# Splitting each weight load of a DeltaNet and hard-swish MLP kernel into two transfers by partition

## The chip, the core and the metric

The kernel runs on one core of one Trainium2 chip. The metric is the device time of one execution in microseconds (us), and the time that counts is the median over several executions. A core has five engines that run side by side, each with its own queue of instructions: TensorE (PE, matrix products; PEld is its loading of the stationary operand), VectorE (DVE), ScalarE (ACT), GpSimd (POOL) and SyncE (SP). SP computes nothing here: it issues transfers between the chip's memory (HBM) and the on-chip buffer, and 16 DMA engines carry them out. The on-chip buffer has 128 partitions; a tile's first dimension lies across them.

## The reference

The inputs `q`, `k`, `v` have 4 batches, 8 heads, 768 positions and 48 features; `beta` has one number for each batch, head and position. The two weight matrices are 64-bit floats: `moe_w_in` is 384 x 2048 and `moe_w_out` is 2048 x 384.

```python
k_n = k / (np.linalg.norm(k, axis=-1, keepdims=True) + 1e-06)
for t in range(S):                                   # per batch and head
    y[:, :, t] = einsum('bhd,bhde->bhe', q[:, :, t], state)
    v_old = einsum('bhde,bhd->bhe', state, k_n[:, :, t])
    state = state + bt * einsum('bhd,bhe->bhde', k_n[:, :, t], v[:, :, t] - v_old)
x = y.transpose(0, 2, 1, 3).reshape(3072, 384)
h = x @ w_in
out = (h * np.clip(h + 3.0, 0.0, 6.0) / 6.0) @ w_out
```

## The kernel before

The recurrence is done in 24 chunks of 32 positions. The four batches of a chunk share the 128 partitions, so a load of a chunk of `k`, `q` or `v` is four transfers of 32 partitions (`load_k`, `load_q`, `load_v`, lines 168, 180 and 193; 48 KB each, in runs of 192 bytes). For each chunk `prep` normalises the keys, turns keys and queries (line 524, evicted by ACT at line 532) and makes the products of keys and queries (line 547, masked by DVE at line 558). A triangular system is solved for the first chunk by small products (`product`, line 596) and for later groups of four chunks by elimination on DVE (lines 730 and 735) that `join` completes (lines 684 to 710). `chain` then carries the state from chunk to chunk. Every two chunks make a block of 256 tokens for the MLP: `up` (line 994) and later `up_by_eleven` (line 1066) multiply by `w_in`, `down` (line 1162) and `down_by_seven` (line 1226) by `w_out`.

The weights arrive as 64-bit floats that no engine multiplies, so they are loaded raw and converted on the chip. They come in 16 pieces, eight of `w_in` and eight of `w_out`. A piece is 128 partitions of 768 numbers, 768 KB raw, and lies on a partition in three runs of 2,048 bytes (`w_in`) or two of 3,072 (`w_out`). `load_w` (line 331) brings one to a raw place: a part of the tile `spare`, or a part of `w_out` that is not yet filled. `scales` (line 356) rebuilds the exponents in four ACT instructions for each piece, and `convert` (lines 378, 383 and 389) does the rest in three DVE instructions. Raw places are used again, so from piece 6 on a load waits until the piece that held its place has been read (`frees`).

The order of all instructions of the first part is written out by hand in the string `ORDER`: `w` stands for the next weight piece, `k`, `q` and `v` for the next transfer of such a load, `a` for the next ACT step of `scales`, `c` for the next DVE step of `convert`. SP issues transfers in this order, one after the other. Each transfer tells of its landing by one of eight semaphores that are handed out in turn, and a semaphore is not used again before its last transfer has landed. So SP stops at a transfer until the one eight places before it (with ACT's own transfers counted) has landed. Around the first pieces the order on SP is: piece 0, six transfers of keys, piece 1, six transfers of keys and queries, piece 2, six more, piece 3, seven more, piece 4. The capital words `K`, `Q`, `V`, `W`, which `do` would hold back behind the last PE instruction, stand in no place of `ORDER`.

```python
320  def load_w(i):
...
331      nc.sync.dma_start(
332          out=raws[i].rearrange("p s f z -> p s (f z)"), in_=src.bitcast(U32)
333      )
...
356  nc.scalar.activation(out=z, in_=z if n else d.bitcast(I16)[:, :, :, 3], func=func, ...)
```

Of the kernel before, what the change touches and what calls it, by code (L numbers as in the profile page):

```python
# [10 lines left out]
U32 = mybir.dt.uint32  # L11
# [33 lines left out]
def kernel(  # L45
# [21 lines left out]
    nc = tc.nc  # L67
# [27 lines left out]
    def rows(b):  # L95
        return slice(C * b, C * b + C)
# [4 lines left out]
    def group(t):  # L101
        return (0, t) if t < G0 else ((t - G0) // GS + 1, (t - G0) % GS)
# [34 lines left out]
    def needs(*what):  # L137
        assert past.issuperset(what), (what, set(what) - past)
# [74 lines left out]
    for j, value in enumerate((1.0, -1.0)):  # L213
        m = mask2[:, j, :]
        for b in range(B):
            nc.gpsimd.memset(mask2[rows(b), j, :], value)
            nc.gpsimd.affine_select(
                out=mask2[rows(b), j, :], in_=mask2[rows(b), j, :], pattern=[[1, C]],
# [95 lines left out]
    raws = []  # L314
    for i, n in enumerate((0, 1, 2, 3, 4, 5, 0, 1, 3, 4, 5, 0, 1, 5, 0, 1)):
        s, f = weights[i][0].shape[1:]
# [3 lines left out]
    def load_w(i):  # L320
        dst, src = weights[i]
        if src.dtype == FP32:
            if i >= NWI:
                needs(("w", NWI - 1))
            nc.sync.dma_start(out=dst, in_=src)
            past.add(("raw", i))
            return
        if i in frees:
            needs(("seen", frees[i], 0), ("seen", frees[i], 1))
        past.add(("raw", i))  # L330
        nc.sync.dma_start(
            out=raws[i].rearrange("p s f z -> p s (f z)"), in_=src.bitcast(U32)
        )

    es = [
        spare[:, 2, j : j + WP * NKT // 2].bitcast(U16).rearrange("p (s f) -> p s f", s=NKT)
# [1016 lines left out]
    def made(name, make, ok=True):  # L1353
        if name not in gens:
            gens[name] = make() if ok else iter(())
        return gens[name]

    def prep_of(t):
        return made(("p", t), lambda: prep(t), t < N)
# [7 lines left out]
    def inverse_of(g):  # L1367
        return made(
            ("i", g), lambda: halves_of(g) if g == 1 else inverse(g), g < NG
        )  # L1370
# [6 lines left out]
    def pieces():  # L1377
        for i in range(NW):
            load_w(i)
            yield  # L1380
# [37 lines left out]
    def behind_tensor(ins):  # L1418
        last = next(
            i for i in reversed(nc.cur_bb.bb.instructions) if i.engine == mybir.EngineType.PE  # L1420
        )
        tc.add_manual_dep(
            ins, last.name,
            mybir.DependencyInfo(mybir.DependencyClass.Sync, mybir.DependencyReason.DATA),
            reason="held back",
        )

    def do(word):
        if word in ("K", "Q", "V", "W"):
            n = len(nc.cur_bb.bb.instructions)  # L1430
            next(gens[word.lower()])
            (new,) = nc.cur_bb.bb.instructions[n:]
            behind_tensor(new)
        elif word in gens:
            next(gens[word])
        elif word[0] == "r":
            relus[word[1]].pop(0)()
        elif word[0] == "g":
            pending[word[1]].pop(0)()
        elif word == "e":  # L1440
            evicts.pop(0)()
        elif word[0] == "i":
            next(inverse_of(int(word[1:])), None)
        else:
            name, t = word[0], int(word[1:])
            if name == "p" and t >= LS + LE:
                next(prep_of(t), None)
            else:
                key = (name, t) if name in "hp" else ("early", name, t)
                next(made(key, lambda: makers[name](t)), None)  # L1450

    with tc.manual_schedule():
        for word in ORDER.split():
            word, _, n = word.partition("*")
            for _ in range(int(n or 1)):
                do(word)
# [12 lines left out]
        for t in range(LS, N):  # L1469
            g, i = group(t)  # L1470
# [93 lines left out]
```

## Time and profile before

| what | value |
|---|---|
| median of 3 runs | 663.58 us (662.71 to 664.91) |
| time of the profiled execution | 662.4 us |
| its span, first to last instruction | 660.6 us |
| PE busy, share of the span | 633.3 us, 96% |
| DVE, ACT, POOL busy | 492.7, 276.7, 217.0 us |
| loads of weight pieces on SP | 16 of 768 KB |
| all transfers issued by SP | 398 |

The span is what the profile sees; the time of the execution is 1.8 us longer, for what lies around it. A page of the profile gives busy time for each engine, the span in 40 slices of 16.5 us, the DMA queues, the chain of work that ended last, groups of instructions by source line, and the DMA issues with the time from issue to landing. A timeline lists instructions as start, duration, engine, line, operation and tile, with the engine's idle time before them and what ended it in square brackets. Where an instruction waits for several things, the view names the one that came last by its own account, which need not be the true one.

### The profile page before, as it was taken

Reading aid. Unit: us, or ns where it says so; the run is one execution under the profiler, and the core shown is the slowest. Engines: PE = TensorE matmul, PEld = TensorE weight load, DVE = VectorE, ACT = ScalarE, POOL = GpSimd, SP = SyncE. Lnnn points to the kernel's source line nnn. Section 1 sums busy time; section 2 is a strip of 40 time slices with the busy share of each in tenths; the row PEclk is TensorE's granted clock in tenths of the full one; section 3 lists DMA queues with packets and bytes.
Section 4 is the critical chain, followed back from the end, with each engine's and each line's share of the span. In section 5 each row is a group of like instructions: output and inputs, shape, how many; then the busy total and the mean of one; then the engine's idle time right before and its main releaser. Section 6 shows DMA issues by size and latency. Waiting matters only on the chain.

```text
span 660.6 us, 26484 instructions
## 1 busy us (share of the span) xinstructions
PE 633.3 (96%) x11592; PEld 567.8 (86%) x11592; DVE 492.7 (75%) x1158; ACT 276.7 (42%) x540; POOL 217.0 (33%) x336
## 2 busy tenths in 40 slices
PE   2768999999999999999999999999999999999997
PEld 2657987776789989999999999999999999999997
DVE  5899877798546698758988848989658998456354
ACT  5897689331243142154144244244244144153250
POOL 6531122003411363553254354164052241331430
PEclk9759999999999999999999999999999999999999
DMA  7888246212140030032030030030020020010000
GB/s 178 209 230 201 76 102 164 45 27 42 27 85 3 12 65 3 2 74 38 2 75 2 3 74 2 3 63 3 2 50 2 2 50 2 14 27 1 26 1 24
DMA packets 88691, 33.27 MB, mean 50 GB/s; under 512 B 80224, under 2 KB 83424, under 8 KB 88576
## 3 DMA queue, kind: packets, MB, share of 16 engines
q1 hardware_dynamic: 88224, 31.29, 21.1%
q8 instruction: 91, 1.49, 0.9%
q10 hardware_dynamic: 352, 0.30, 0.2%
q14 instruction: 24, 0.20, 0.1%
HBM read 26.84 MB, written 4.72 MB: 48 GB/s over the span
## 4 chain that ended last, share of the span: by engine, by line
PE 92%; ACT 3%; DVE 2%; DMA 2%; SPq 1%; issue 0%; ACTq 0%; DVEq 0%
PE po L1226 28%; PE ph L1066 24%; PE ph L994 12%; PE po L1162 6%; PE ks L806 4%; PE pt L524 3%; PE py L827 3%; PE pz L827 3%; PE sc L547 3%; PE su L938 3%; ACT spare L356 2%; DMA kf<-in_k_dram 1%; PE yt L873 1%; PE pi L684 1%; DVE pr L730 1%; DVE A L735 0%
## 5 line engine op out<-in xcount | busy, mean ns | idle before, releaser
L1066 PE MATMUL ph<-xT,w_in 128*128 128x128 f32 (+1 forms) x640 | 139.0, 321 | 0.0
L1226 PE MATMUL po<-w_out,g 128*128 128x192 f32 x640 | 110.6, 326 | 0.0
L1066 PEld LDWEIGHTS ph<-xT,w_in 128*128 128x128 f32 x640 | 104.0, 191 | 5.9
L1030 POOL TENSOR_TENSOR g<-g 128x256 f32<-128x256 f32 (+1 forms) x128 | 78.3, 613 | 92.8 <-ACT g L1080 87.8
L1226 PEld LDWEIGHTS po<-w_out,g 128*128 128x128 f32 x640 | 104.6, 190 | 0.5
L994 PE MATMUL ph<-xT,w_in 128*128 128x256 f32 (+1 forms) x480 | 93.3, 343 | 1.5 <-DVE g L1004 1.0
L1226 PE MATMUL po<-spare,g 128*128 128x192 f32 x480 | 86.7, 332 | 0.0
L994 PEld LDWEIGHTS ph<-xT,w_in 128*128 128x128 f32 x480 | 76.2, 190 | 11.5 <-DVE g L1004 1.3
L1226 PEld LDWEIGHTS po<-spare,g 128*128 128x128 f32 x480 | 77.2, 190 | 1.8
L1080 ACT ACTIVATE g<-ph 128x512 f32<-128x512 f32 x64 | 38.2, 597 | 92.8 <-PE ph L1066 92.8
L1236 POOL TENSOR_TENSOR o<-o,u 128x192 f32<-128x192 f32 x18 | 13.7, 762 | 165.9 <-ACT o L1233 87.9
L759 DVE TENSOR_TENSOR pr<-A 128x30 f32<-128x30 f32 (+9 forms) x150 | 58.8, 392 | 3.1
L1093 DVE TENSOR_TENSOR g<-ph,g 128x256 f32<-128x256 f32 x64 | 26.8, 419 | 44.4 <-PE ph L1066 39.5
L1212 DVE TENSOR_TENSOR g<-g 128x512 f32<-128x512 f32 x80 | 56.3, 724 | 4.6 <-PE po L1226 4.5
L764 DVE TENSOR_TENSOR A<-A,pr 128x30 f32<-128x30 f32 (+9 forms) x150 | 56.0, 373 | 3.5
L1001 ACT ACTIVATE g<-ph,halves 128x256 f32<-128x256 f32 (+1 forms) x80 | 33.7, 428 | 56.7 <-PE ph L994 56.7
L356 ACT ACTIVATE spare<-spare,places 128x768 uint16<-128x768 uint16 (+1 forms) x56 | 52.5, 942 | 2.3 <-DMA kf<-in_k_dram 1.2
L1113 DVE SCALAR_TENSOR_TENSOR g<-o,g 128x512 f32<-128x512 f32 x64 | 46.4, 725 | 6.8 <-ACT o L1110 6.8
L1110 ACT ACTIVATE o<-g,halves 128x512 f32<-128x512 f32 x64 | 46.2, 723 | 10.5 <-DVE g L1113 7.8
L1066 PE MATMUL ph<-beta_tok,sums_in 128*128 128x128 f32 x256 | 49.5, 275 | 0.0
L1233 ACT ACTIVATE o<-po 128x192 f32<-128x192 f32 x40 | 13.2, 330 | 82.9 <-PE po L1226 79.3
L510 POOL TENSOR_TENSOR kb<-kf,inv 128x384 f32<-128x384 f32 x24 | 21.7, 905 | 74.0 <-issue 43.1
(141 smaller groups left out, 1022.0 us busy)
## 6 DMA issues: line engine op xcount, KB each, us to landing
kf<-in_k_dram SPq DMA_DIRECT2D x96, 48.0 KB, 2.5
qb<-in_q_dram SPq DMA_DIRECT2D x96, 48.0 KB, 2.7
vf<-in_v_dram SPq DMA_DIRECT2D x96, 48.0 KB, 2.0
out_dram<-o SPq DMA_DIRECT2D x90, 48.0 KB, 1.6
spare<-in_moe_w_in_dram SPq DMA_DIRECT2D x4, 768.0 KB, 5.3
w_out<-in_moe_w_in_dram SPq DMA_DIRECT2D x4, 768.0 KB, 5.6
w_out<-in_moe_w_out_dram SPq DMA_DIRECT2D x4, 768.0 KB, 7.4
spare<-in_moe_w_out_dram SPq DMA_DIRECT2D x4, 768.0 KB, 5.0
```

What stands on the lines that cost most here:

```text
L356: nc.scalar.activation(out=z, in_=z if n else d.bitcast(I16)[:, :, :, 3], func=func, bias=places[:, n : n + 1], scale=scale,)
L759: nc.vector.tensor_tensor(out=pv, in0=A[:, j + 1 :, j].unsqueeze(2).to_broadcast([n, w, j]), in1=A[:, j, 0:j].unsqueeze(1).to_broadcast([n ...
L764: nc.vector.tensor_tensor(out=A[:, j + 1 :, 0:j], in0=A[:, j + 1 :, 0:j], in1=pv, op=ALU.subtract)
L827: nc.tensor.matmul(ps[rows(place(b)), D * h : D * h + D], lhsT=m(h)[rows(b)], rhs=z[rows(b), D * at(h) : D * at(h) + D], start=True, stop= ...
L994: nc.tensor.matmul(ph[:, cols], lhsT=w_in[:, s, f * 128 : (f + 1) * 128], rhs=xT[:, s, cols], start=(s == 0), stop=(s == NKT - 1),)
L1030: nc.gpsimd.tensor_tensor(out=out, in0=a, in1=b, op=op)
L1066: nc.tensor.matmul(ph[:, n], lhsT=w, rhs=x, start=start, stop=stop, skip_group_check=True)
L1110: nc.scalar.activation(out=r, in_=g, func=ACTF.Relu, bias=half, scale=1.0 / 6.0)
L1113: nc.vector.scalar_tensor_tensor(out=g, in0=r, scalar=1.0, in1=g, op0=ALU.min, op1=ALU.mult)
L1162: nc.tensor.matmul(pos[c][:], lhsT=gs[blk, f // 2][:, f % 2, c * P : (c + 1) * P], rhs=w_out[:, f, :], start=(f == 0), stop=(f == NFC - 1),)
L1212: nc.vector.tensor_tensor(out=A(f, *out, 4), in0=A(f, *a, 4), in1=A(f, *b, 4), op=op)
L1226: nc.tensor.matmul(ps[n][:], lhsT=A(f - f % 2, *a)[:, f % 2], rhs=b[:, f], start=(f == 0), stop=(f == HF - 1),)
```

## The change

`load_w` issues two transfers for a piece in place of one. For even pieces the first takes partitions 0 to 119 and the second 120 to 127; for odd pieces the first takes 0 to 71 and the second 72 to 127. Places, bytes and runs within a partition stay the same. The other edit is in `do`, where the dependence of a held-back word is put on the first new instruction instead of the only one; no word of `ORDER` uses it. On PE, DVE, ACT and POOL the order of instructions is the same as before; on SP the 16 weight loads become 32 transfers, each pair side by side, so 398 transfers become 414.

```diff
@@ def load_w(i)
-        nc.sync.dma_start(
-            out=raws[i].rearrange("p s f z -> p s (f z)"), in_=src.bitcast(U32)
-        )
+        n = 72 if i % 2 else 120
+        for r in (slice(0, n), slice(n, 128)):
+            nc.sync.dma_start(
+                out=raws[i][r].rearrange("p s f z -> p s (f z)"), in_=src[r].bitcast(U32)
+            )
@@ def do(word)
-            (new,) = nc.cur_bb.bb.instructions[n:]
-            behind_tensor(new)
+            behind_tensor(nc.cur_bb.bb.instructions[n])
```

## The prediction

> **What bounds the kernel now.** I read the table of stretches first (start and end; length; busy time of PE, PEld, DVE, ACT and POOL with instruction counts; clock, DMA share, GB/s), to see where a later landing could matter.
>
> ```profile
> 0.00:12.00 12.00, 3.10 (x72) 2.51 (x72) 5.61 (x22) 4.33 (x8) 7.96 (x34) 1.00 0.67 148
> 12.00:43.00 31.00, 20.85 (x675) 17.54 (x672) 26.37 (x60) 27.25 (x38) 14.66 (x19) 0.69 0.92 219
> 43.00:60.00 17.00, 12.44 (x313) 10.97 (x313) 16.00 (x46) 13.80 (x24) 2.26 (x5) 0.87 0.94 233
> 60.00:660.60 600.60, 596.90 (x10535) 536.80 (x10535) 444.74 (x1032) 231.36 (x472) 192.11 (x278) 1.00 0.16 35
> ```
>
> From 60 us on PE is busy for 596.9 of 600.6 us; the table of waits for that part holds only one for PE, the 0.9 us that ends at 60.24. Whatever moves that instant moves the end by as much, and a load that lands late after it has to be very late. Before it the DMA engines are over 0.9 busy and ACT works 27.25 of 31 us. So the start-up alone is at stake. There I read what SP issues and what ACT does with the pieces (timelines of SP and of ACT):
>
> ```profile
> 6.65 0.45 SPq L331 DMA_DIRECT2D spare<-in_moe_w_in_dram  x1
> 7.14 2.95 SPq L168 DMA_DIRECT2D kf<-in_k_dram  x6
> 10.14 0.45 SPq L331 DMA_DIRECT2D spare<-in_moe_w_in_dram  x1
> 11.95 0.31 SPq L180 DMA_DIRECT2D qb<-in_q_dram  x1
> ...
> 14.78 0.45 SPq L331 DMA_DIRECT2D w_out<-in_moe_w_in_dram  x1
> ...
> 19.69 0.45 SPq L331 DMA_DIRECT2D w_out<-in_moe_w_in_dram  x1
> 21.46 0.81 SPq L180 DMA_DIRECT2D qb<-in_q_dram  x2
> ```
> ```profile
> 12.01 2.92 ACT L356 ACTIVATE spare<-spare,places 128x768 uint16<-128x768 int16 x3 [1.20 <-DMA kf<-in_k_dram]
> 15.51 1.80 ACT L356 ACTIVATE spare<-spare,places 128x768 uint16<-128x768 uint16 x2
> 21.56 1.01 ACT L356 ACTIVATE spare<-w_out,places 128x768 uint16<-128x768 int16 x1
> 26.93 0.98 ACT L356 ACTIVATE spare<-w_out,places 128x768 uint16<-128x768 int16 x1
> 34.22 0.98 ACT L356 ACTIVATE spare<-w_out,places 128x768 uint16<-128x768 int16 x1
> 38.48 0.99 ACT L356 ACTIVATE spare<-w_out,places 128x768 uint16<-128x768 int16 x1
> ```
>
> The view of single transfers gives issue to landing for pieces 0, 1, 3 and 4 as 5.3, 5.3, 6.0 and 5.2 us, so they land at 11.94, 15.4, 25.7 and 30.9. Piece 2 is seen by SP, which stops from 20.14 until 21.46 for it: 6.7 us. Piece 5, issued at 31.56, holds SP until 38.41: 6.8 us. ACT takes them up at 12.01, 16.4 (the second of the pair at 15.51), 21.56, 26.93, 34.22 and 38.48. Cover of pieces 0 to 5: 0.1, 1.0, 0.1, 1.2, 3.3 and 0.1 us. ACT waits for a landing only at 12.01 (1.20 us; the label names keys, but the instruction reads piece 0). At pieces 2 and 5 it arrives just as they do. ACT is in order and the turned keys and queries (L532) go through it, so a late piece holds up the recurrence.
>
> **Part 1: how many engines a transfer gets.** ACT's queue holds four transfers of 8 partitions (beta), and six of 32 partitions (output):
>
> ```profile
> q1 hardware_dynamic: 88224, 31.29, 21.1%
> q8 instruction: 91, 1.49, 0.9%
> q10 hardware_dynamic: 352, 0.30, 0.2%
> spare<-in_beta_dram ACTq DMA_DIRECT2D x4, 24.0 KB
> out_dram<-o ACTq DMA_DIRECT2D x4, 24.0 KB, 1.5
> out_dram<-o ACTq DMA_DIRECT2D x2, 48.0 KB, 1.8
> ```
>
> Their runs are 4 x 8 + 6 x 32 = 224 packets. The other 128 of the 352 are completions: 4 x 8 + 6 x 16. So 8 partitions went to 8 engines, 32 to 16. An engine count that divides the partitions fits both; 120 then gets 15 engines with 8 rows (partitions) each, 72 gets 12 with 6, 56 gets 14 with 4. If every transfer starts at the same first engine, the busiest carries 8 + 1 = 9 rows of an even piece and 6 + 4 = 10 of an odd one, against 8 now. Bounds: no extra row if the split is even over 16, two if it is as said; I take one for even and two for odd pieces.
> The Trainium skill states this rule ("DMA: Bandwidth & Descriptors", on why a DMA increments its semaphore by 16): the largest count up to 16 that divides the slowest dimensions, and the lowest-numbered engines. The trace agrees for 8 and 32; no row shows 120, 72 or 56.
>
> Price of a row: 16 rows, one on each engine, are 98,304 bytes. In the window 8 to 10 us, almost all piece 0, the rate is 242 GB/s, 0.41 us; the best window, 28 to 30, has 358 GB/s, 0.27 us. I take 0.3 for one row and 0.7 for two.
>
> **Part 2: SP's order and its eight semaphores.** Sixteen more issues of 0.45 us are SP's time; SP has idle gaps, so alone I cost them at 0.3 us (0 to 0.5 for each pair, covered by the landing that SP waits for anyway). The places count for more. Between pieces 0 and 1 stand six key transfers. With 0a, 0b, six keys, 1a, piece 1a is exactly eight behind 0a and cannot be issued before 0a has landed. The same holds for 2a behind 1a and 3a behind 2a; 4a is eight behind 3b. Before, piece 1 left at 10.14 while piece 0 was under way. Behind each held piece wait the key and query loads that follow it on SP.
>
> **The sum.**
> - Piece 0: second part one row behind the first, ACT starts +0.3 (0 to 0.4).
> - Piece 1: issued at 11.95 (+1.8), 5.3 us plus at most 0.7: lands 17.2 to 17.9. ACT wants it at 16.7. But ACT idles 1.06 us before the squaring (L407) at 18.37, which takes up most; ACT stands at +0.4 after it.
> - Piece 2: leaves when 1a lands, four rows (1.4 us) before all of piece 1, at 16.5 (+1.7). With 5.3 + 0.3 to 6.7 + 0.3 us it lands 22.1 to 23.5, wanted at 22.0: 0.1 to 1.5 late, middle 0.8. ACT at +1.2.
> - Piece 3: leaves when 2a lands, about 22.5; 5.2 to 6.0 plus 0.7 us: 28.4 to 29.2, wanted at 28.1; middle 0.7 late. ACT at +1.9.
> - Piece 4: leaves at 28.8, lands 34.3, wanted at 36.1: covered. Were that gone, it would cost what it is late.
> - Piece 5: it left 5.8 us after piece 4 before; now 28.8 + 0.5 + 5.8 = 35.1, landing 41.1 to 42.6, wanted at 40.4. I take the lower end, +0.7, as fewer loads stand before it on the engines: ACT at +2.6.
> - Pieces 6 and later are cost at nothing: piece 6 lands at 42.2 and is wanted at 44.19, and while DVE eliminates (48.7 to 57.7) ACT has gaps. If that cover went, one more us.
>
> Total +2.6 us, ends 0.7 (pieces 2, 3 and 5 nearly covered) and 5.1 (all upper ends). The profiled execution's 662.4 becomes 665.0. The median of the runs stands 1.2 above it (663.58), which gives 666.2.
>
> **Rivals.**
> *Nothing to see (0 to +2.0, about 664.4).* Rows cost less if HBM sets the rate rather than the engines: fewer engines then run faster each, row cost near 0, and pieces land at the lower ends: +0.7 to +1. For: rates vary from 133 to 358 GB/s between windows of equal DMA share. Against: DMA shares at 0.9 and above. That the transfers spread evenly after all belongs here.
> The Trainium skill's rules for kernel authors on the same page say not to split a transfer by partitions, since the parts share the engines and serialize; by that alone the time would be no better, at least +0.3. No run so far shows a split.
>
> *Faster, by a late engine (661.1).* Queue q8 reads instructions: 91 packets for 0.9% of 16 engines' span, 95 us, so about 1.0 us on one engine each time. Pieces 2 and 5 took 1.4 us longer than 0 and 1; one engine held up by such a read would do that. If these reads fall on engines that the splits leave out or spare, pieces and the loads behind them land up to 1.4 us sooner and the held issues are paid back. But ACT waited only 1.20 us for a landing, so a gain over that needs more: the clock. From 24 to 46 us the windows show PE at 0.50. The chain has 9.4 us of PE work there (1.19, 1.86, 1.06, 1.28, 1.91 and 2.07), and four turns took 0.63 us at full clock (22.09) against 1.11. Were the clock kept, up to 4 us go; I price it at 2.5. It decides if loads land early enough to close PE's gaps of 1.11 and 1.90 us at 21.35 and 24.61. Against: these gaps end on DVE and ACT, not on a load.
>
> **How the numbers follow.** This kernel's measurement tells about 0.3%, 2 us, from no change. Forecast case (pieces serialized, +2.0 to +5.1, 665.6 to 668.7): 0.48. Nothing to see: 0.30, plus 0.02 of the late engine with a small gain: 0.32. Late engine with the clock: 0.20. The range 661.0 to 668.7 leaves out about half of the last case and the tail above.
>
> **What would show it.** In the profile after: q1 has 88,360 packets (each even piece 15 + 8 completions for 16, each odd one 12 + 14; +136), 88,480 if all split transfers used 16 engines. Piece 1's first part is issued near 12, piece 2's near 16.5, piece 3's near 22.5. ACT shows new waits before L356 at pieces 2, 3 and 5, and PE's wait of 0.9 us ends near 62.8 instead of 60.24, with the same 600 us behind it. The prediction is wrong if ACT's steps stay in place, if PE gets there earlier, or if the time behind that instant changes.

## The result, and the profile after

The changed kernel takes 683.65 us (median of 6 runs, 681.82 to 686.0) where the kernel before takes 663.84 (6 runs): a ratio of 1.029 (1.028 to 1.031), 20 us slower. The forecast was 666.2 with an upper end of 668.7. The direction was right, the size wrong by a factor of nearly eight (+20 for +2.6). The profiled execution took 681.94 us with a span of 680.2.

The table of stretches of the changed kernel comes first, with the columns of before (start and end; length; busy time of PE, PEld, DVE, ACT and POOL; clock, DMA share, GB/s).

```profile
12.00:43.00 31.00, 17.12 (x582) 14.12 (x586) 22.34 (x54) 22.20 (x31) 10.80 (x18) 0.97 0.93 159
43.00:60.00 17.00, 9.07 (x298) 7.30 (x287) 8.92 (x14) 10.82 (x15) 3.12 (x4) 0.54 0.87 152
60.00:100.00 40.00, 31.72 (x919) 28.67 (x920) 30.69 (x91) 23.39 (x50) 4.37 (x9) 0.96 0.69 142
100.00:200.00 100.00, 99.86 (x1818) 73.97 (x1819) 76.22 (x183) 48.31 (x85) 22.99 (x30) 1.00 0.35 67
```

The third stretch in the kernel before:

```profile
60.00:100.00 40.00, 39.76 (x1333) 35.51 (x1334) 32.53 (x82) 30.54 (x63) 8.28 (x12) 1.00 0.41 101
```

Read the last two columns. From 12 to 43 us the DMA engines are as busy as before (0.93, before 0.92) but move 159 GB/s where it was 219; from 43 to 60 us it is 152 for 233. PE, DVE and ACT do less in the same time. PE, which was full from 60.24 us on, is now short by 8.3 us between 60 and 100 (31.72 of 40; before 39.76) and full only after that. So the loss is one of the start-up, as forecast, but the start-up has become longer.

PE has the same 11,592 matrix products in the same order in both traces, so each can be compared with itself. Those that ran at 25, 50, 70 and 100 us before run 4.5, 11.7, 18.7 and 19.3 us later, and the one at 300 us still 19.2. The delay builds up in steps while pieces 0 to 11 are loaded; nearly all of it is there before piece 12 leaves, at 91.18 us. Of the span's 19.6 us, PE's busy time brings 3.9 (637.2 for 633.3; the granted clock is now low from 43 to 60 us, 0.54, where it was from 12 to 43, 0.69; what that does to the 3.9 is not shown). The other 15.7 are idle time of PE.

The DMA queue that carries SP's transfers, changed kernel (packets, MB, share of 16 engines' span):

```profile
q1 hardware_dynamic: 88360, 31.29, 23.6%
```

The packet count is the forecast one to the last: 15 + 8 completions for an even piece, 12 + 14 for an odd one. The bytes are the same, but the packets took 23.6% of 680.2 us, 160.5 us for each engine, where they took 21.1% of 660.6, 139.4. That is 21 us of engine time for no byte more. The trace's records of single packets say which: a weight packet of 2,048 bytes took 84 ns in the median before and 140 now, one of 3,072 bytes 121 before and 205 now. The weight packets make 13 of the 21 us (54.9 for 41.7). Another 7 are packets of 192 bytes (85.4 for 78.0), the loads of keys, queries and values, whose shape nobody changed.

SP's timeline of the changed kernel:

```profile
6.89 0.86 SPq L333 DMA_DIRECT2D spare<-in_moe_w_in_dram  x2
7.79 2.79 SPq L168 DMA_DIRECT2D kf<-in_k_dram  x6
13.16 0.97 SPq L333 DMA_DIRECT2D spare<-in_moe_w_in_dram  x2
...
18.53 1.83 SPq L333 DMA_DIRECT2D w_out<-in_moe_w_in_dram  x2
...
25.97 0.76 SPq L333 DMA_DIRECT2D w_out<-in_moe_w_in_dram  x2
26.77 0.88 SPq L180 DMA_DIRECT2D qb<-in_q_dram  x2
```

And what ACT waited for in the first 60 us (waited in total, times, longest):

```profile
ACT spare L358 <- DMA w_out<-in_moe_w_in_dram: 8.5, 4, 4.9
...
ACT spare L358 <- DMA kf<-in_k_dram: 3.2, 1, 3.2
ACT spare L358 <- DMA spare<-in_moe_w_in_dram: 2.8, 2, 1.8
```

The pieces leave as part 2 of the prediction has it, each once the first part of the last has landed, but at 13.16, 18.53 and 25.97 where 11.95, 16.5 and 22.5 were forecast. All transfers are later than the semaphores alone make them. ACT, which waited 1.20 us for a piece before, now waits 14.5 (8.5 + 3.2 + 2.8); piece 5 alone, which landed at 49.0 in place of 38.4, costs 4.9.

PE also stops in the middle of groups of like products. The reason given is `issue`, the view's word for waiting for nothing that the profile shows:

```profile
38.73 0.84 PE L549 MATMUL sc<-KQ 64*32 64x64 f32 x62 [0.69 <-ACT KQ L534]
41.29 0.29 PE L549 MATMUL sc<-KQ 64*32 64x64 f32 x2 [1.73 <-issue]
...
44.23 1.27 PE L940 MATMUL su<-R,sums_in 32*64 32x48 f32 x61 [0.58 <-ACT R L929]
47.33 0.45 PE L940 MATMUL su<-R,sums_in 32*64 32x48 f32 x3 [1.83 <-issue]
```

And in the table of PE's waits from 60 us on:

```profile
PE pz L829 <- issue: 2.7, 1, 2.7
PE su L940 <- issue: 2.2, 1, 2.2
```

The four stops make 8.5 of the 15.7 us of idle time; in the kernel before, none in the first 130 us is longer than 0.3. Each ends 1.3 to 1.6 us after a packet of q8, the queue that reads instructions, has ended (at 39.80, 45.71, 79.30 and 85.38). The traces of all kernels that do the whole computation have 37 such stops of over 0.5 us in the first 130 us, and all end 1.3 to 1.9 us after such a packet. So part of the loss looks like PE running out of instructions because their reads come late while loads crowd the DMA engines. The traces do not say whose instructions a packet carries or what held it up, so this path is argued, not shown.

### The profile page after: what moved, and what is told of

The parts are those of the page before. It is cut to its first block, busy times and chain, and to the rows that moved or that the text cites. A ratio compares the mean times of both kernels' runs of the same rounds, so it can differ in the third digit from the quotient of the medians.

```text
span 680.2 us, 26506 instructions
## 1 busy us (share of the span) xinstructions
PE 637.2 (94%) x11592; PEld 570.0 (84%) x11592; DVE 492.7 (72%) x1158; ACT 277.5 (41%) x540; POOL 215.4 (32%) x336
## 3 DMA queue, kind: packets, MB, share of 16 engines
q1 hardware_dynamic: 88360, 31.29, 23.6%
## 4 chain that ended last, share of the span: by engine, by line
PE 87%; DMA 8%; DVE 2%; SPq 1%; issue 1%; ACT 1%; ACTq 0%; DVEq 0%
PE po L1228 28%; PE ph L1068 23%; PE ph L996 12%; PE po L1164 6%; DMA spare<-in_moe_w_in_dram 4%; PE ks L808 4%; DMA w_out<-in_moe_w_in_dram 3%; PE pz L829 3%; PE py L829 3%; PE su L940 3%; PE pt L526 3%; PE sc L549 2%; PE yt L875 1%; DMA vf<-in_v_dram 1%; PE pi L686 1%
## 5 line engine op out<-in xcount | busy, mean ns | idle before, releaser
L996 PE MATMUL ph<-xT,w_in 128*128 128x256 f32 (+1 forms) x480 | 95.3, 348 | 1.9 <-DVE g L1006 1.2
L1238 POOL TENSOR_TENSOR o<-o,u 128x192 f32<-128x192 f32 x18 | 13.7, 764 | 166.1 <-ACT o L1235 87.7
L1095 DVE TENSOR_TENSOR g<-ph,g 128x256 f32<-128x256 f32 x64 | 26.8, 419 | 44.9 <-PE ph L1068 40.3
```

What stands on the lines that cost most here:

```text
L996: nc.tensor.matmul(ph[:, cols], lhsT=w_in[:, s, f * 128 : (f + 1) * 128], rhs=xT[:, s, cols], start=(s == 0), stop=(s == NKT - 1),)
```

## The experiments

Three theories stood. A: the packets themselves got slower, since two engines write at the same time through one way into the buffer. B: SP's eight semaphores hold the pieces back. C: the busiest engine has one or two rows more.

**Shapes alone on the chip.** Only loads of a weight piece, one after the other, in various shapes.

```diff
+ SHAPES = [[FULL], [slice(0, 120)], [FULL], [slice(120, 128)], ..., [slice(0, 120), slice(120, 128)], ...]
+ for shapes in SHAPES:
+     for r in shapes:
+         nc.sync.dma_start(out=raw[r]..., in_=w_in[...][r].bitcast(U32))
```

> Left out: the whole computation; SP only issues loads of one weight piece in various shapes, one after the other (each waits for the one before, since both write the same tile), three times over. Theory A, two engines on one path: in the trace of the changed kernel a packet of 2,048 bytes takes a median of 140 ns against 84 before, many of them 160 to 168, twice 84, so two engines write at the same time to partitions that share a way into the buffer. If rows are dealt to engines in blocks and partitions 32 apart share a way, then alone on the chip 128 partitions take 84 ns a packet, 120 and 64 partitions about 168, 96 and 112 between (some packets 84, some 168), the first 8 partitions about 336 (8 engines on two ways), partitions 0, 4, 8 to 28 from the same source rows 84 again, partitions 0 to 7 from source rows 0, 4, 8 to 28 again 336. The Trainium skill's page 'SBUF — State Buffer', section 'Door 1: The DMA port swizzle', has such a map: four neighbours and the four 32 further on share one of 16 ports. Theories B (SP's eight semaphores hold back the pieces) and C (the busiest engine has one or two more rows): every shape takes 84 ns a packet, and landing differs only by the rows on the busiest engine.

Packets of 2,048 bytes had a median of 138 ns for 120 partitions and 84 for all other single loads, from 8 to 128; as pairs, 120 with 8 had 142, 72 with 56 112, 64 with 64 146 and 112 with 16 105. That fits neither side as written: C and B had 84 for all, A had 168 for 64 and 336 for 8. Taken in order, though, the packets of the 64-partition load, issued alone, run at 84 ns at first (some eight on each engine) and then at 155 to 168 to its end. So what slows them comes in only after some 16 KB on each engine, and short loads can't show it. The run left A open and asked for a longer one.

**Two halves, 112 and 16, and the place alone.** The first two cut by partition so that both parts have all 16 engines and no engine has an extra row; the third has whole pieces and only the second place on SP.

```diff
-        n = 72 if i % 2 else 120
+        n = 64        # other kernel: n = 112
```
```diff
+        nc.sync.dma_start(out=raws[i]..., in_=src.bitcast(U32))                    # 128 partitions
+        nc.sync.dma_start(out=slots[0:1, i : i + 1], in_=k[0, 0, 0:1, i : i + 1])  # 4 bytes
```

> Every piece as 64 and 64 partitions. Both parts get 16 engines and 4 rows each, so no engine carries more than before, and SP has the same 32 weight transfers as the changed kernel. Theory A (two engines on one path): blocks of 4 rows put engines e and e + 8 on partitions 32 apart, all packets of the pieces take twice 84 ns; the packet time of the weights goes from 41.7 us for each engine to some 80, 690 to 705 us. Theory B (semaphores): as the changed kernel or a little better, 675 to 684. Theory C (extra rows): none here, 663 to 665.

> Every piece as 112 and 16 partitions, 7 rows and 1 row on each of 16 engines. Theory A: blocks of 7 rows let only about 4 of 16 engines share a path at a time and 16 rows are one eighth of the piece, so most packets are back at 84 ns: 666 to 675 us. Theory B: the same order on SP as in the changed kernel, 678 to 684. Theory C: no extra row, 663 to 665.

> Every piece as one transfer of 128 partitions again, followed by a load of 4 bytes to a place that nobody reads, so SP's order and the use of the eight semaphores are those of the changed kernel and the weight packets those of before. Theory B: 675 to 684 us. Theories A and C: 663.5 to 668, what the places and 16 more issues cost (my sum for them alone was 1 to 3 us).

Measured, beside 664.70 for the kernel before: 678.37 (ratio 1.021, 1.019 to 1.023), 673.99 (1.014, 1.011 to 1.017) and 666.96 (1.0037, 1.0024 to 1.0050). The place alone costs 2.3 us, so B is real and small. 64 and 64, with nothing that C could charge, costs 13.7. That lies in the range written for B, but the place alone was to cost as much by B (675 or over) and does not. A expected more for it (690 or over), as if every packet were slowed; in its trace the packets of 2,048 bytes have piece medians from 116 to 166 ns, so a part of them is still spared by the slow start seen above. For 112 and 16 they are at 84 in six of eight pieces; those of 3,072 bytes are at 140 to 206 there and at 154 to 238 with 64 and 64.

The run with 4 bytes is also a test of the prediction's part 2 by itself. Its SP timeline:

```profile
6.66 0.45 SPq L333 DMA_DIRECT2D spare<-in_moe_w_in_dram  x1
...
11.93 0.39 SPq L333 DMA_DIRECT2D spare<-in_moe_w_in_dram  x1
...
17.17 0.39 SPq L333 DMA_DIRECT2D w_out<-in_moe_w_in_dram  x1
...
22.63 0.39 SPq L333 DMA_DIRECT2D w_out<-in_moe_w_in_dram  x1
...
28.16 0.79 SPq L333 DMA_DIRECT2D w_out<-in_moe_w_in_dram  x1
...
35.24 0.45 SPq L333 DMA_DIRECT2D w_out<-in_moe_w_in_dram  x1
```

The forecast for pieces 1 to 5 was 11.95, 16.5, 22.5, 28.8 and 35.1, and for the whole +2.6 us, in which the price of rows is contained; for places and issues alone the text above this run has 1 to 3.

**Ways in, measured by themselves.** Long loads (48 KB for a partition, packets of 16,384 bytes) to chosen partitions, each followed by one of 128 partitions.

```diff
+ WAYS = [(slice(0, 8), slice(0, 8)), (slice(0, 32, 4), slice(0, 8)), (slice(0, 64, 8), slice(0, 8)), ...,
+         (slice(0, 8), slice(0, 32, 4)), ..., (slice(0, 64), slice(0, 64)), ...]   # (partitions, source rows)
+ for to, at in WAYS:
+     nc.sync.dma_start(out=raw[to], in_=w_in[at].bitcast(U32))
```

> Left out: the whole computation; SP issues loads of whole rows of the input weights (48 KB for a partition, in packets of up to 16 KB), one after the other, to chosen partitions; after each a load of 128 partitions. In the shapes alone an engine kept 84 ns for 2,048 bytes over its first 8 or so packets and slowed to about 165 only later, so short loads don't show the effect and these long ones should. Theory A (partitions that are neighbours in fours, or 32 apart, share one way in, and a way carries what one engine brings): 8 source rows on 8 engines take about 2.0 us of data when they go to partitions 0, 4, 8 to 28, twice that (4.0) to 0, 8, 16 to 56 and to 0, 16, 32 to 112, and four times (8.0) to 0 to 7, from whichever source rows. 16 rows: 4.0 to 0, 4 to 60 and to 0, 8 to 120, 8.0 to 0 to 15. 64 rows 16 us where 4 rows on each engine would take 8; 120 rows up to 32; 128 rows 16. Rival A2, the source side (rows of the memory 16 KB apart): the time goes by the source rows and the partitions written make no difference, all 8-row loads from rows 0 to 7 equal. Theory C (rows on the busiest engine): 2 us for each row on an engine, whatever the partitions.

The table of stretches of this run, inside loads of 128, 64, 112 and 120 partitions in this order (nothing computes, so the columns before the clock are empty; the last two are DMA share and GB/s):

```profile
330.00:345.00 15.00, 0.00 (x0) 0.00 (x0) 1.00 0.97 411
511.00:526.00 15.00, 0.00 (x0) 0.00 (x0) 1.00 0.98 205
546.00:566.00 20.00, 0.00 (x0) 0.00 (x0) 1.00 1.02 255
586.00:616.00 30.00, 0.00 (x0) 0.00 (x0) 1.00 0.91 190
```

The engines are about as busy in all four (0.91 to 1.02) and move 411, 205, 255 and 190 GB/s. 64 partitions take as long (15.2 us) as 128 (15.4), and 120 twice that (30.8). The packet medians are 611 ns for 128, 1,280 for 64, about 1,100 for 112 and 1,285 for 120. For 8 source rows, dealt to 8 engines, the partitions written decide. In the second of two rounds: 2.3 us to 0, 4 to 28; 3.5 to 0, 8 to 56 and 3.6 to 0, 16 to 112; 6.0 to 0 to 7 (median packet 2,252 ns). Sent to 0 to 7 from source rows 0, 4 to 28 it is 6.8. Sixteen rows: 3.9 to 0, 4 to 60, 3.7 to 0, 8 to 120, 6.7 to 0 to 15, where the median packet is 2,420 ns, four times 611.

So a way carries what one engine brings, 16,384 bytes in 611 ns or 26.8 GB/s, and two or four engines on it get a half or a quarter each. Rival A2 fails, since loads from the same source rows differ by a factor of 2.6 between two sets of partitions. C fails too: 8 rows on 8 engines are one row each in all of these. The Trainium skill's map ("SBUF — State Buffer", "Door 1: The DMA port swizzle": 16 ports, four neighbours and the four 32 further on share one) gives one, two and four engines on a way in these loads; the packet times of 611, 1,280 and 2,420 ns agree.

The trace does not record which engine moved a packet, but the packet times tell how rows are dealt. With 120 partitions in blocks of 8, engine e writes from partition 8e on, and engines 0, 4, 8 and 12 start at 0, 32, 64 and 96: two and two on one way, at all times, as measured. Dealt in turn (partition 0 to engine 0, 1 to 1 and so on), four neighbours would meet, and the packets would be at 2,420. A load of all 128 partitions is dealt otherwise, since its packets never meet.

**One ratio for all pieces.**

```diff
-        n = 72 if i % 2 else 120
+        n = 120       # other kernel: n = 72
```

> Every piece as 120 and 8 partitions. In the changed kernel the packets of even pieces (120 and 8) were the slower ones, 3.6 us of packet time for each engine against 3.3 for odd ones and 2.6 before. Theory A: slower than the changed kernel, 686 to 692 us. Theory C: one extra row everywhere in place of one and two, so faster than it, 676 to 682. Theory B alone: 667.

> Every piece as 72 and 56 partitions. Theory A: its packets were the less slow ones, so faster than the changed kernel, 676 to 682 us. Theory C: two extra rows everywhere, so slower than it, 686 to 692. Theory B alone: 667.

685.52 us (ratio 1.029, 1.024 to 1.034) and 678.47 (1.017, 1.011 to 1.024), beside 665.35 for the kernel before. The order is A's: 120 and 8, with one extra row but two engines on a way throughout, is the dearer one; 72 and 56, with two extra rows, is cheaper by 7 us. The first lies 0.5 us below A's range, the second inside it. A also expected 120 and 8 to be slower than the changed kernel; the two are alike (+20.2 and +19.8). That a kernel with half its pieces cut each way costs as much as the dearer way is not explained.

**The same two transfers, cut within the partition.**

```diff
-        n = 72 if i % 2 else 120
-        for r in (slice(0, n), slice(n, 128)):
-            nc.sync.dma_start(out=raws[i][r]..., in_=src[r].bitcast(U32))
+        for r in (slice(0, 1), slice(1, None)):
+            nc.sync.dma_start(out=raws[i][:, r], in_=src[:, r].bitcast(U32))
```

> Every piece as two transfers again, but cut within the partition: one run of each partition in the first, the rest in the second, 128 partitions in both. SP's order, the number of transfers, the places of the eight semaphores and the bytes are those of the changed kernel, and each engine has the partitions that it had before. Theory A: packets back at 84 and 121 ns and the time at 665 to 669, as with the load of 4 bytes (666.96). Rival, that two transfers for a piece cost so much however they are cut: 674 to 684.

666.89 us, a ratio of 1.0018 (0.9997 to 1.0039). Its queue:

```profile
q1 hardware_dynamic: 88480, 31.29, 20.5%
```

20.5% of a span of 665.4 is 136.4 us for each engine, where the changed kernel has 160.5 and the kernel before 139.4. This is the run that settles it: as many transfers, at the same places, and 18 us of the 20 are gone once both parts have all 128 partitions. The 1.5 us that are left lie between nothing and the 2.3 of the place alone, and the interval (0 to 2.6 us) holds both.

**Where the time enters.** The change made for pieces 0 to 5 alone, and for 10 to 15 alone.

```diff
+        n = (72 if i % 2 else 120) if i < 6 else 128      # other kernel: if i >= 10
+        for r in (slice(0, n), slice(n, 128))[: 2 if n < 128 else 1]:
```

> Pieces 0 to 5 split as in the changed kernel, 6 to 15 whole. What is tested is where the time enters. The prediction's step: pieces 6 and later cost nothing, so this has nearly all of it, 681 to 685 us. Against it, theory A with the 16 engines as the limit of the whole crowded stretch: in the changed kernel piece 5 landed 9.4 us later than before (47.8 for 38.4) and piece 11 23.4 later (85.9 for 62.5), so the first six bring about 8 to 9 and the rest comes after them: 670 to 675.

> Pieces 10 to 15 split as in the changed kernel, 0 to 9 whole. The prediction's step: no cost, 663.5 to 665.5 us. Theory A: pieces 10 and 11 are still in the crowded stretch, 12 to 15 come when the engines have gaps, so a little: 666 to 669.

Beside 665.59: 674.79 (ratio 1.0139, 1.0123 to 1.0156), +9.2 us, inside A's range and far below the 681 of the prediction's step; and 669.82 (1.0050, 1.0025 to 1.0074), +4.2. The first six pieces bring nearly half, the last six a fifth; what the four between bring was not measured by itself, the sum leaves about 6. Neither group is free, and the second lies 0.8 us above A's range. In its trace PE stops at `issue` for 1.5 us until 71.82 and for 1.9 until 106.25, each time 1.4 to 1.6 us after a packet of q8.

**Extra rows by themselves.** Whole pieces, each followed by a copy of 48 or 96 KB to an unused place in the chip's memory, dealt to 8 engines: one or two rows more on each of 8 engines, and nothing written to the buffer.

```diff
+        nc.sync.dma_start(out=more[i], in_=moe_w_in.rearrange("(s p) f -> p s f", p=128)[0:8, :, 0:256]...)   # or 0:512
```

> Every piece as one transfer of 128 partitions, followed by a copy of 48 KB from weights to an unused place in the chip's memory, dealt to 8 engines with three packets of 2,048 bytes each: the place and the semaphore of a second part, and one row more on each of 8 engines, with nothing written to the buffer. Beside the load of 4 bytes (666.96 us), which has the place alone, the difference is the price of one extra row on the busiest engines. Theory C: 0.25 to 0.4 us for each of the dozen pieces in the crowded stretch, 3 to 5 us more: 670 to 672. Theory A alone, if rows cost nothing: 666 to 668.

> As the run with one extra row, with rows of twice the bytes: two rows more on each of 8 engines. Theory C: twice the difference, 673 to 677 us. Theory A alone: 666 to 668.

666.53 (ratio 1.0033, 1.0015 to 1.0052) and 666.64 (1.0038, 1.0019 to 1.0057) beside 664.50. That is +2.0 and +2.1, the price of the place (2.3) and nothing for the rows that shows beside intervals of 1.2 us to either side. Their 16 small copies moved at 84 ns for 2,048 bytes and 159 for 4,096. C is out as a term of its own. What stays open is whether an extra row costs more when its packets are slow: 112 and 16 has nearly the packet time of the changed kernel (23.6% of 673.7, 159.0 us for each engine) without extra rows and is 10 us faster, and 64 and 64 has more (24.4% of 677.5, 165.3) and costs 6 us less. So packet time summed over the engines does not by itself order the costs. Nor do PE's stops at `issue` (over 0.5 us, first 130 us): 13.1 us for 120 and 8, 11.2 for 72 and 56, 8.5 for the changed kernel, 8.1 for 64 and 64, 7.3 for 112 and 16, but 1.8 for the place alone and 1.3 for the cut within the partition. Both are large where the cost is large and small where it is small.

**A try at a better version.** If the loads of 32 partitions, two engines on each of eight ways, are limited by the ways, taking the batches in turn from both halves of the buffer should help the kernel before.

```diff
-            for b in range(B):
+            for b in (0, 2, 1, 3):       # load_k, load_q, load_v
```

> The kernel before with the four transfers of each load of keys, queries and values in the batch order 0, 2, 1, 3. A load of 32 partitions has 16 engines on 8 ways, batches 0 and 1 on the one eight and 2 and 3 on the other; taken alternately, what waits at one way could drain while the next transfer uses the others. If that limits these loads (192 bytes in 15 ns for each of two engines on a way is 25.6 GB/s, near the 26.8 of a full way in the long loads: 16,384 bytes in 611 ns), the crowded stretch gets shorter and the time falls to 655 to 662 us. If each packet of 192 bytes costs its 15 ns anyway: same time, 663 to 666.

665.01 us beside 665.59, a ratio of 0.9995 (0.9979 to 1.0010): no difference. Nothing that was run beats the kernel before.

## Why the prediction was wrong, point by point

- **What is at stake: right.** All of the loss arises in the first 100 us, and PE's order and the time behind it stay as they were. It ends later than forecast: PE's wait that ended at 60.24 ends at 73.52, where 62.8 was forecast, and PE then stops twice more, until 86.84.
- **Part 2, SP's order and semaphores: right in mechanism.** With the place alone, pieces 1 to 5 leave within 0.7 us of the forecast times, and the cost is 2.3 us. That it lies so near to the sum's 2.6 is in part luck, since the sum also holds prices of rows, and rows alone measured nothing beyond the noise.
- **Part 1, engine counts: right.** The queue has the forecast 88,360 packets.
- **Part 1, the price: the step that failed.** The prediction bounded a split transfer by its rows, none to two at 0.27 to 0.41 us, and took each packet to be as fast as before. Rows alone measured nothing (+2.0 and +2.1 for one and two, with the place). The term that mattered was not there: which partitions an engine writes. A weight packet went from 84 to 140 ns and from 121 to 205, and all packets together from 139.4 to 160.5 us for each engine. With 128 partitions in both parts they take 136.4, and 18 of the 20 us are gone. The bound from both sides was one on the count of rows only; that a transfer of another shape may have another speed was excluded without a reason. The forecast took the rate of windows with whole pieces (242 to 358 GB/s); of the long loads of 64 partitions and more, 128 partitions are the one shape that is spared.
- **Pieces 6 and later at nothing: failed.** Pieces 10 to 15 alone cost 4.2 us. Their cover was taken from the landing times before, as if late pieces left the next ones where they were. But the landings fall back further and further: 1.9 us at piece 0 (13.8 for 11.9), 10.6 at piece 5 (49.0 for 38.4), 23.5 at piece 11 (86.0 for 62.5). (The text ahead of the run with the first six pieces has 47.8 and 85.9; those two miss the last completion.) And no term stands for PE's stops at `issue`: two of 1.5 and 1.9 us in the trace of pieces 10 to 15 alone, 8.5 us in that of the changed kernel.
- **Piece 12 and the capital `W`.** The section on the kernel before says that no capital word stands in `ORDER`. One does, a `W`, and it loads piece 12. That load waits for PE in both kernels and leaves at 72.28 us before and at 91.18 after, so it follows PE's delay and does not make it. The other edit, in `do`, serves this load.
- **The sum of piece 0: an early sign.** Its second part was to land 0.3 us behind and landed 1.9 later than the whole piece did before, although only 0.2 us of that is a later start (6.89 for 6.65).
- **Rivals.** "Fewer engines then run faster each" is refuted by the long loads: 15 engines moved 190 GB/s, 16 on whole pieces 411. The late engine brought no gain; if the instruction reads played a part, it was the other way round, as reads that came late for PE. The Trainium skill's advice not to split by partitions ("DMA: Bandwidth & Descriptors", the rules for kernel authors), which the prediction set at 0.3 us or more, pointed the right way. Its reason, that the parts share the engines and serialize, does not account for the loss here: two parts of 128 partitions share them as well and cost 1.5 us, two of 64 cost 13.7.

## What to carry to other kernels

Before changing the shape of a transfer, ask not only how many engines carry it but which partitions they write at the same time, and price it with a packet time of its own, measured on a long load. The sign here was a DMA share that stayed at 0.93 while GB/s fell from 219 to 159. Where a load must be cut, cut along the partition and leave all 128 partitions in each part. And where the DMA engines are crowded, reckon cover from the new landing times and not from the old, and look for stops of PE at `issue`, which a list of late loads does not show.

## What the hardware showed that was not expected

- A transfer of 64 partitions takes as long as one of 128 (15.2 and 15.4 us with 48 KB for each partition), and 120 partitions take twice as long (30.8).
- In a load that runs alone the slowdown comes only after some eight packets of 2,048 bytes on an engine: the first of a load of 64 partitions run at 84 ns, the later ones at 155 to 168. Eight rows written to eight neighbouring partitions, three such packets each, show nothing (84 ns). Short measurements miss it.
- In the kernel before, the packets of pieces 9 and 10 are slow too, 156 and 153 ns for 3,072 bytes in the median where the other pieces of that size have 121; with the place alone both have 121. The cause was not followed up.
- PE's stops at `issue` of over 0.5 us, 37 in the first 130 us of twelve traces, all end 1.3 to 1.9 us after a packet of the queue that reads instructions. In the kernel before there are none.
